# A fused scan and feed-forward kernel: masks of the second pair issued early, scores put into the differences' banks, two constants moved, one weight clamp issued ahead of a hidden block

## The chip, the cores and the metric

One core of a Trainium2 chip. The metric is the device time of one execution in microseconds; a median is of several executions. The engines are called PE (TensorE), DVE (VectorE), ACT (ScalarE), POOL (GpSimd) and SP (SyncE, which here only issues transfers).

## The reference, cut to what matters

A chunked state-space scan over 768 positions (4 batches, 8 heads of 32, state 16), whose output, reshaped to 3072 tokens of 256, goes through a feed-forward layer with a quick GELU:

```python
cum = np.cumsum(log(clip(a)), axis=-1)
L = np.exp(cum[..., :, None] - cum[..., None, :]) * causal
M = np.einsum('bhin,bhjn->bhij', Cc, Bc) * L          # scores times decays
y = M @ x + (C @ state) * exp(cum)                    # within and across chunks
...                                                    # state is carried from chunk to chunk
h = x @ w_in                                           # 256 x 2048
out = (h / (1 + exp(-1.702 * h))) @ w_out              # 2048 x 256
```

The weights are 64-bit floats. The kernel reads them as pairs of 32-bit words and makes 32-bit floats of them itself.

## The kernel before

The scan runs over pairs of 128-position chunks. For a pair, `mask` writes the causal mask into a PSUM bank, `differ` adds the differences of `cum` to it (32-row products, one group of rows per `r`), `decay_exp` takes the exponent on ACT, `score` computes C times B, `weigh` multiplies the two on DVE, `turn_only` transposes b and c, `ends` forms Be and `since_start` CsT (b and C weighted with decays), `gain` and `keep` advance the state, `finish` forms y.

```python
own = const.tile([P, HB, D], FP32, name="own")
nc.gpsimd.tensor_tensor(out=own, in0=same[:, :HB], in1=same[:, HB:], op=ALU.add)
idents = const.tile([P, NH, P], FP32, name="idents")
nc.gpsimd.tensor_copy(idents, ident.unsqueeze(1).to_broadcast([P, NH, P]))
```

A weight piece is decoded in four steps, three on DVE and one on ACT. Pieces 0 to 5 are `w_in`, 6 to 9 are `w_out`; piece 6 is the first 1 MB of `w_out`:

```python
def fields(i):   # DVE, L157 and L160: exponent bits, mantissa bits
def clamp(i):    # ACT, L168 and L169: two Relus over the exponent
def rounded(i):  # DVE, L173: adds the low word
def join(i):     # DVE, L184 and L190: sign, product into w_in or w_out
    ...
    for n in NEXT.get(i, ()):      # NEXT = {1: (6,), 4: (7,), 5: (8,), 7: (9,)}
        fetch(n)                   # loads piece n into the buffer that join(i) freed
def narrow(i):
    rounded(i); fields(i + 1); join(i)
```

All loads named here are issued by SP in program order:

```python
for i in range(1, 4): fetch(i)
rows_a(az, (nc.sync,))
for i in range(4, 6): fetch(i)
load(PG)              # b, c and x of the third pair: six strided loads
spread_rows(1)        # rows of a
# ... and, where join(1) stands in the program, fetch(6)
```

The start, with what the change touches:

```python
for r in range(R):
    ab[0, r] = ab0[:, r]; mask(ab[0, r])
idle = bank("idle")
for i in range(4):
    mask(idle)                       # filler: keeps PE busy, result unused
differ(0, ...); exps(0, range(R)); turn_only(0, ...)
fields(0); clamp(0); rounded(0)
score(0)
for r in range(2):
    ab[1, r] = bank(f"ab1_{r}"); mask(ab[1, r])
differ(1, ...); exps(1, range(2))
ends(0, 0, nc.gpsimd); ends(0, 1, nc.gpsimd)
weigh(0); turn_only(1, ...); gain(0)
...                                  # masks 2 and 3, differences, exponents
since_start(0, nc.gpsimd)            # CsT on POOL
since_start(1, nc.gpsimd)
keep(0); join(0); fields(1); rounded(1)
...                                  # score(1), weigh(1), y of pair 0
half(0, 0)                           # first half hidden block
weigh(1, (1,)); finish(1, late=True); join(1)
half(1, 0); keep(1, (1,))
fields(2); clamp(2)
load(PG + 1)
```

After that come the other half blocks (`half`), full hidden blocks 4 to 15 (`hidden`, L654), and the projection (`o`, L766), which needs `w_out`'s first piece decoded.

## Time and profile before

| | before |
|---|---|
| median | 377.97 us (3 runs, 377.84 to 378.61) |
| profiled span | 376.0 us, clock full |
| PE busy | 98% of the span |
| first scores | 10.38 us |
| first half hidden block | 20.42 us |
| block eight (behind PE's last wait of the first 60 us) | 37.66 us |
| block twelve | 46.70 us |
| first projection | 54.11 us |
| last PE operation | 371.52 us |

Between the two stands one more input, `w_out`'s first piece. These are SP's issues that lead to it (columns: start and duration in us, queue, line, operation):

```profile
17.46 6.48 SPq L119 DMA_DIRECT2D b<-in_B_dram  x2
23.98 3.89 SPq L119 DMA_DIRECT2D c<-in_C_dram  x2
27.92 1.25 SPq L119 DMA_DIRECT2D x<-in_x_dram  x2
29.21 0.79 SPq L222 DMA_DIRECT2D af<-in_a_dram  x1
30.13 0.37 SPq L145 DMA_DIRECT2D bits<-in_moe_w_out_dram  x1
```

The buffer for the piece is free once `join(1)` has read it, by 23.92 at the latest, but SP issues the load at 30.13, because until 29.17 it is at the third pair's b, c and x. Not all of that is issuing. SP's own waits from 12 to 34 us hold this line (total us, times, longest):

```profile
SPq L119 <- DMA bits<-in_moe_w_in_dram: 4.1, 2, 3.0
```

SP waits twice for an earlier piece of `w_in` to land, 1.1 us before b's first load and 3.0 between its two, so the 6.48 us above contain 3.0 of waiting. In the built program the loads count on eight semaphores in turn, and each waits until the load eight places ahead of it has landed. The piece landed at 38.44, and DVE's `fields(6)` started at 39.37 without a wait: 0.9 us of slack, which no list of waits shows.

### The profile page before, as it was taken

Reading aid. Unit: us, or ns where it says so; the run is one execution under the profiler, and the core shown is the slowest. Engines: PE = TensorE matmul, PEld = TensorE weight load, DVE = VectorE, ACT = ScalarE, POOL = GpSimd, SP = SyncE. Lnnn points to the kernel's source line nnn. Section 1 sums busy time; section 2 is a strip of 40 time slices with the busy share of each in tenths; the row PEclk is TensorE's granted clock in tenths of the full one; section 3 lists DMA queues with packets and bytes.
Section 4 is the critical chain, followed back from the end, with each engine's and each line's share of the span. In section 5 each row is a group of like instructions: output and inputs, shape, how many; then the busy total and the mean of one; then the engine's idle time right before and its main releaser. Section 6 shows DMA issues by size and latency. Waiting matters only on the chain.

```text
span 376.0 us, 5774 instructions
## 1 busy us (share of the span) xinstructions
PE 367.3 (98%) x2282; PEld 284.5 (76%) x2282; DVE 268.4 (71%) x439; ACT 152.2 (40%) x337; POOL 12.4 (3%) x35
## 2 busy tenths in 40 slices
PE   8999999999999999999999999999999999999995
PEld 3674458876457678878888878888878888888884
DVE  4889999996879998677887564888574355544343
ACT  5668643402332122554333454333454331454330
POOL 6200000000000010000000000000000000000000
PEclk9999999999999999999999999999999999999999
DMA  9989788624848100077300064000010000000011
GB/s 152 240 255 204 169 300 120 156 98 83 200 87 177 58 15 27 2 126 154 108 6 0 3 104 121 0 2 0 0 58 2 0 3 1 0 2 0 0 58 56
DMA packets 85795, 29.56 MB, mean 79 GB/s; under 512 B 75721, under 2 KB 79241, under 8 KB 85769
## 3 DMA queue, kind: packets, MB, share of 16 engines
q1 hardware_dynamic: 83320, 28.81, 32.9%
q10 hardware_dynamic: 2448, 0.39, 0.6%
q8 instruction: 18, 0.29, 0.3%
q14 instruction: 9, 0.07, 0.1%
HBM read 25.95 MB, written 3.24 MB: 78 GB/s over the span
## 4 chain that ended last, share of the span: by engine, by line
PE 93%; DVE 3%; ACT 2%; DMA 1%; issue 1%; ACTq 0%; DVEq 0%
PE acc L823 32%; PE X L726 15%; PE Y L736 11%; PE h L654 11%; PE o L766 8%; PE cb L539 3%; PE y L612 3%; PE y L603 2%; PE tp L496 2%; PE ab L460 1%; PE oT L857 1%; PE h L668 1%; PE A L567 1%; DMA az<-in_a_dram 1%; DVE p L184 1%
## 5 line engine op out<-in xcount | busy, mean ns | idle before, releaser
L823 PE MATMUL acc<-mg,mw 128*128 128x256 f32 x240 | 65.4, 379 | 0.0
L731 ACT ACTIVATE ac<-X 128x256 f32<-128x256 f32 x64 | 24.6, 384 | 68.9 <-PE X L726 68.8
L654 PE MATMUL h<-yT,w_in 128*128 128x512 f32 x112 | 50.3, 596 | 0.9 <-DVE w_in L190 0.8
L823 PEld LDWEIGHTS acc<-mg,mw 128*128 128x128 f32 x240 | 45.6, 190 | 6.2
L840 DVE TENSOR_TENSOR gT<-Y,ac 128x512 f32<-128x512 f32 x32 | 22.1, 692 | 38.0 <-PE Y L736 34.9
L703 ACT ACTIVATE gT<-gT 128x512 f32<-128x512 f32 x64 | 33.3, 520 | 28.5 <-DVE gT L840 28.5
L823 PE MATMUL acc<-gT,w_out 128*128 128x256 f32 x160 | 43.8, 380 | 0.0
L352 DVE TENSOR_TENSOR_SCAN L<-a,idents 128x1024 f32<-128x1024 f32 x18 | 41.1, 2283 | 0.0
L654 PEld LDWEIGHTS h<-yT,w_in 128*128 128x128 f32 x112 | 20.7, 190 | 24.9 <-issue 22.9
L726 PE MATMUL X<-my,mi 128*128 128x256 f32 x128 | 38.7, 384 | 0.0
L823 PEld LDWEIGHTS acc<-gT,w_out 128*128 128x128 f32 x160 | 30.1, 190 | 5.4 <-issue 1.4
L840 DVE TENSOR_TENSOR gT<-Y,b 128x256 f32<-128x256 f32 x32 | 13.5, 422 | 28.0 <-PE Y L736 27.7
L657 ACT ACTIVATE gT<-h 128x512 f32<-128x512 f32 x28 | 16.5, 596 | 39.7 <-PE h L654 39.7
L550 DVE TENSOR_TENSOR L<-L,cb 128x2048 f32<-128x2048 f32 (+1 forms) x13 | 27.6, 2121 | 5.7 <-PE cb L539 5.5
L766 PE MATMUL o<-w_out,gT 128*128 128x256 f32 x128 | 29.3, 383 | 0.0
L694 DVE TENSOR_TENSOR mg<-gT 128x512 f32<-128x512 f32 x40 | 27.3, 683 | 1.9 <-ACT gT L703 1.9
L726 PEld LDWEIGHTS X<-my,mi 128*128 128x128 f32 x128 | 23.8, 190 | 4.2 <-issue 1.2
L766 PEld LDWEIGHTS o<-w_out,gT 128*128 128x128 f32 x128 | 23.8, 190 | 4.1 <-issue 0.7
L823 PE MATMUL acc<-gT,mw 128*128 128x256 f32 (+1 forms) x86 | 24.0, 368 | 0.4 <-DVE c L840 0.4
L823 PE MATMUL acc<-mg,w_out 128*128 128x256 f32 x80 | 23.5, 379 | 0.0
L634 ACT ACTIVATE yT<-y 128x256 f32<-128x256 f32 x22 | 7.2, 381 | 36.7 <-PE y L612 35.5
L736 PE MATMUL Y<-yT,mi 128*128 128x256 f32 x64 | 19.5, 386 | 0.0
(142 smaller groups left out, 540.9 us busy)
## 6 DMA issues: line engine op xcount, KB each, us to landing
a<-scratch SPq DMA_DIRECT2D x18, 512.0 KB, 5.5
bits<-in_moe_w_out_dram SPq DMA_DIRECT2D x4, 1024.0 KB, 7.1
x<-in_x_dram SPq DMA_DIRECT2D x24, 128.0 KB, 3.1
out_dram<-ob SPq DMA_DIRECT2D x11, 256.0 KB, 2.2
bits<-in_moe_w_in_dram SPq DMA_DIRECT2D x4, 512.0 KB
bits<-in_moe_w_in_dram SPq DMA_DIRECT2D x2, 1024.0 KB
b<-in_B_dram SPq DMA_DIRECT2D x24, 64.0 KB, 3.8
c<-in_C_dram SPq DMA_DIRECT2D x22, 64.0 KB, 2.8
```

The costliest lines, as they stand in the source:

```text
L352: nc.vector.tensor_tensor_scan(out=Ls[p][:, k].rearrange("p r q i -> p (r q i)"), data0=ra[n], data1=idents.rearrange("p h i -> p (h i)"), ...
L550: nc.vector.tensor_tensor(out=Lv[:, k], in0=Lv[:, k], in1=cb.rearrange("p r k e -> p k r e")[:, k], op=ALU.mult)
L654: nc.tensor.matmul(out=h, lhsT=w_in[:, k, f * P:(f + 1) * P], rhs=yT[g][:, k], start=(k == 0), stop=(k == NK - 1))
L657: nc.scalar.activation(gT[g, j][:, i], h, AF.Silu, scale=GELU_SCALE)
L694: nc.vector.tensor_tensor(out=t[:, 0:2], in0=B[:, :, 1], in1=B[:, 0], op=ALU.subtract)
L703: nc.scalar.activation(o, i, AF.Silu, scale=GELU_SCALE)
L726: nc.tensor.matmul(out=s["X"], lhsT=lhsT, rhs=rhs, start=i == "1", stop=i == "4", skip_group_check=True)
L731: nc.scalar.activation(copy, s["X"], AF.Copy)
L736: nc.tensor.matmul(out=o, lhsT=lhsT, rhs=rhs, start=s.pop("new", False), stop=i != "5", skip_group_check=True)
L766: nc.tensor.matmul(out=o[k // 2][:, k % 2], lhsT=gT[g, f // 2][:, f % 2, k * P:(k + 1) * P], rhs=w_out[:, f], start=(f == 0 and k % 2 == 0 ...
L823: nc.tensor.matmul(out=acc[g][0][i][:, cols], lhsT=lhsT, rhs=rhs[:, cols], start=(j == 0 and i in (0, 2, 5, 6)), stop=(j == NF // 2 - 1), ...
L840: nc.vector.tensor_tensor(out=o, in0=v, in1=w, op=ALU.add)
```

## The change

Its intent: take the second pair's first two masks off PE's path between scores and differences by issuing them where filler products stood; write the first scores over the four banks of the first differences, with another order of row groups; move two POOL constants away from the start, where they hold up DVE's scans; and issue `clamp(2)` on ACT ahead of the half block's Silu.

```diff
     own = const.tile([P, HB, D], FP32, name="own")
-    nc.gpsimd.tensor_tensor(out=own, in0=same[:, :HB], in1=same[:, HB:], op=ALU.add)
     idents = const.tile([P, NH, P], FP32, name="idents")
-    nc.gpsimd.tensor_copy(idents, ident.unsqueeze(1).to_broadcast([P, NH, P]))
@@ score
-    def score(p):
+    def score(p, to=None):
-        cb = area(f"cb{p}").rearrange("p r (k e) -> p r k e", k=2)
-        for k in range(2):
-            for r in range(R):
+        cb = (area(f"cb{p}") if to is None else to).rearrange("p r (k e) -> p r k e", k=2)
+        for k, r in [(k, r) for r in range(R) for k in range(2)] if to is not None else [
+                (k, r) for k in range(2) for r in range(R)]:
@@ the start
+    for r in range(2):
+        ab[1, r] = bank(f"ab1_{r}")
+        mask(ab[1, r])
     idle = bank("idle")
-    for i in range(4):
+    for i in range(2):
         mask(idle)
@@
-    score(0)
-    for r in range(2):
-        ab[1, r] = bank(f"ab1_{r}")
-        mask(ab[1, r])
+    score(0, ab0)
     differ(1, [(r, ab[1, r]) for r in range(2)])
     exps(1, range(2))
+    nc.gpsimd.tensor_tensor(out=own, in0=same[:, :HB], in1=same[:, HB:], op=ALU.add)
@@
     since_start(1, nc.gpsimd)
+    nc.gpsimd.tensor_copy(idents, ident.unsqueeze(1).to_broadcast([P, NH, P]))
@@
     join(1)
+    fields(2)
+    clamp(2)
     half(1, 0)
     keep(1, (1,))
-    fields(2)
-    clamp(2)
```

In the changed kernel most lines below 331 have a number lower by three: L654 is L651, L766 is L763, L460 is L457. The decoding lines (L157 to L190) keep theirs.

More of the change, by code (lines that the diff above doesn't have):

```diff
@@ L529, in scores @@
         weigh(p)
-    def score(p):
+    def score(p, to=None):
         s = st[p]
         BT, CT = s.pop("BT"), s.pop("CT")
-        cb = area(f"cb{p}").rearrange("p r (k e) -> p r k e", k=2)
-        for k in range(2):
-            for r in range(R):
-                rows = slice(32 * r, 32 * r + 32)
-                nc.tensor.matmul(out=cb[:, r, k], lhsT=BT[rows, k],
-                                 rhs=CT[rows, k].rearrange("p q i -> p (q i)"),
-                                 start=True, stop=True, tile_position=(32 * r, 0),
-                                 skip_group_check=True)
+        cb = (area(f"cb{p}") if to is None else to).rearrange("p r (k e) -> p r k e", k=2)
+        for k, r in [(k, r) for r in range(R) for k in range(2)] if to is not None else [
+                (k, r) for k in range(2) for r in range(R)]:
+            rows = slice(32 * r, 32 * r + 32)
+            nc.tensor.matmul(out=cb[:, r, k], lhsT=BT[rows, k],
+                             rhs=CT[rows, k].rearrange("p q i -> p (q i)"),
+                             start=True, stop=True, tile_position=(32 * r, 0),
+                             skip_group_check=True)
         s["cb"] = cb
```

## The prediction

> **What bounds the kernel now.** I read the page first (TensorE, PE, is busy 98% of 376.0 us), then the list of PE's waits over the whole span, then the chain of waits of the first 60 us, then the timeline there. PE's waits:
>
> ```profile
> PE busy L378 <- DVE ones L258: 1.2, 1, 1.2
> PE h L654 <- DVE w_in L190: 0.8, 1, 0.8
> PE ab L460 <- DVE cum L292: 0.7, 1, 0.7
> PE cb L539 <- DVE C L503: 0.5, 1, 0.5
> PE h L668 <- ACT y L634: 0.4, 1, 0.4
> PE acc L823 <- DVE c L840: 0.4, 1, 0.4
> ```
>
> All but the last, which is in the tail, fall before 37.66 us. From there PE streams without a wait to the tail, so the change is worth exactly what it moves the eighth hidden block (the first L654 matmul after the 0.8 us wait, at 37.66), unless the earlier PE then meets a wait that was hidden. The chain of waits (start, us, what) that leads there:
>
> ```profile
> 10.38 1.15 PE cb L539 x16
> 11.52 0.54 PE ab L452 x2
> 12.06 1.93 PE ab L460 x16
> 13.99 0.59 PE tp L496 x4
> ...
> 24.27 1.94 PE h L668 x8
> 26.20 0.02 issue
> 26.23 0.60 ACT gT L672
> 26.82 0.62 ACT p L168
> 27.44 0.02 issue
> 27.47 0.73 ACT p L169
> 28.20 0.02 issue
> 28.22 0.70 DVE p L184
> ...
> 36.29 1.24 DVE w_in L190
> 37.52 0.14 issue
> 37.66 3.67 PE h L654 x8
> ```
>
> Two stretches matter. Up to 24 us PE itself sets the pace with small matmuls, two masks (L452) among them. From 26.2 us the chain leaves PE: ScalarE (ACT) does a Silu, only then the clamp of weight piece 2 (L168, L169), for which VectorE (DVE) idles 1.63 us at L184. DVE then decodes pieces 2, 3, 4 nearly without a gap until PE has to wait for piece 4.
>
> **What the Trainium skill says.** (1) "SBUF — State Buffer", section "SBUF: two separate sides": DVE and GpSimd (POOL) share one port pair under an exclusive lock, held for a whole instruction, against DVE operations with two SBUF inputs or in a two-port mode; the other blocks fully. The trace agrees:
>
> ```profile
> 5.12 0.46 POOL L331 TENSOR_TENSOR own<-same 128x128 f32<-128x128 f32 x1
> 5.22 2.28 DVE L292 TENSOR_TENSOR_SCAN cum<-carry,cum 128x256 f32<-128x256 f32 x2 [0.48 <-ACT cum L287]
> 5.52 1.43 POOL L334 COPY idents<-ident 128x1024 f32<-128x1024 f32 x1
> ```
>
> The two scans last 908 and 1452 ns by the view of their line, while a scan of the same size at 48.2 us, L447, takes 691 ns. The first is held about 0.22 us (by own), the second about 0.76 us (by idents). (2) "TensorEngine Tiling (Array Packing)", "Key Properties": changing the tiling mode drains TensorE. Here masks use all 128 rows and their neighbours 32-row tiles, so both edges of the masks cost. (3) "TensorE: Matmul & The Clock Gate", Part 3, says matmuls stay in strict order. This trace disagrees across row groups: the second scores (L539) start at 16.44, while differences (L460), earlier in program order on other row groups, still start at 16.64, 16.86 and 17.08. So a row group can run ahead of another. (4) "ScalarE: Activation LUTs", "What ACT_TABLE_LOAD costs", gives 1283 ns for a load; the one before the first y copies took 1.28 us. The change leaves it.
>
> **The change part by part.** The built instruction orders tell more than the diff.
>
> *Masks.* Filler products on identical operands become the second pair's first two masks: eight products before the first scan as before (4 + 2 + 2 instead of 4 + 4), two fewer in all. They finish before cum arrives (6.18 us), so moving them costs nothing. At 11.45 the two masks vanish. Rounds of 32-row passes start 0.216 us apart (16.43, 16.64, 16.86, 17.08 above). The scores' last round starts at 10.38 + 0.32 + 2 x 0.216 = 11.13 (first round 0.32 with its exposed load), so the differences can start at 11.34 rather than 11.99, and without their own 0.10 us of first-load gap: 0.65 + 0.10 = 0.75 us. The rest follows: transposes 13.17 (was 13.92), A 13.76, second half's differences 14.71, their exponents on ACT 16.74 to 17.83 (were 17.49 to 18.58). The loads for those transposes land near 12 us, early enough.
>
> *Scores into the differences' banks.* In the program before, these were already the same four banks, and the first score waited for the fourth exponent (10.32). In the changed program the wait has the same values. So no wait goes. The new order (two products of one row group in a row) puts up to four passes of one group ahead of the next; the overtaking seen at 16.44 covers just about that depth. I count 0.
>
> *own.* On POOL nothing stands between its old and new place: same position, 0.
>
> *idents.* From 5.52 to behind the second CsT on POOL (16.53 before, about 15.8 now). The second scan gets 0.76 us faster, which nobody waits for: its readers start at 8.71 (the rows product). At the new place DVE works without a gap on two-SBUF-input or two-port operations (join 0, fields 1, rounded 1). Join 0's last operation would end at 17.80 - 0.75 = 17.05, idents then holds the lock 0.8 us, and rounded(1) ends at about 19.27 instead of 19.20. So DVE loses there all of the 0.75 us that the masks gave it.
>
> *Result at the first hidden blocks.* A(1) waits for DVE's Be (19.6 + 0.07), the y copies for ACT (early now). First hidden matmul: A(1) last issued near 19.9, then a change of mode, about 20.0 instead of 20.42, so 0.4 earlier. The next hidden block (24.19 before) needs join 1, which ended at 23.92 and now ends at 23.99: about 24.05, so 0.15 earlier. The halves that follow run until 29.48 - 0.15 = 29.33.
>
> *fields(2), clamp(2) ahead of the half.* ACT does clamp 2 directly behind the y copies: 24.54 to 25.92, instead of 26.72 to 28.19 behind the Silu. DVE runs fields 2, state, rounded 2, fields 3 to 26.53 and then join 2 without the 1.63 us wait: done at 27.86 instead of 29.64. The first full hidden block starts at PE's own 29.33 (was 29.79). Clamp 3 stays behind the Silu of the half that PE ends near 28.0: clamp 3 is done at 29.94. Join 3 then runs 29.97 to 31.38 (was 32.77), rounded 4 and fields 5 to 33.72, join 4 (1.22 + 1.23) to 36.12 instead of 37.51. PE arrives at 29.33 + 6.94 = 36.27 (four blocks took 29.79 to 36.30 for the last start, plus 0.43); join 4 plus its 0.146 us latency is 36.27 as well. Block eight: 36.28 instead of 37.66, so 1.38 us earlier. The 0.8 us wait disappears; the rest is PE's own start.
>
> *Sum.* Masks +0.75, idents -0.6 (of its 0.83 on DVE, what PE feels), leaving 0.15 at 24 us; clamp order adds about 1.2; scores, own 0: total 1.38. Behind it the slacks are: first projection at 54.11 against join 6 done at 53.57 (0.54 us). DVE is one gapless chain there, and fields 6 needs w_out's first piece, which landed near 38.4 whatever PE does, so DVE may come only about 0.9 earlier: join 6 near 52.70 plus 0.15, against PE's 52.73. That may give back 0.1. I predict 1.3 us.
>
> **The rivals.** *A: the lock costs nothing.* If idents slips in while DVE reads PSUM (the weighing L550, one SBUF input), then DVE keeps its 0.75 and PE reaches block eight about 0.5 earlier still: 1.8 to 1.9 us, 376.1. Against: DVE reads SBUF twice for 2 us just when POOL is free. *B: the new score order breaks the overlap of row groups.* Sixteen passes of which each group's four run alone would take about 2.8 us instead of 1.15 (an estimate: 13 steps of 0.216, since only the edges overlap); the differences come about 1.6 later, the mask gain is lost and DVE's first weighing, which starts at 12.00 now, waits too. With the clamp order still helping: 378 to 378.5. Against: the overtaking above. *C: the gain is given back behind 38 us* by a w_out piece or its load: 0.3 to 0.6 us kept, 377.5. For: 0.54 us of slack, and DMA is 90% busy in many slices until 45 us. Against: the DVE chain moves earlier as well. *D: the decode was bound by loads, not by ACT*: pieces 4 and 5 landed near 25 and 27.5, their fields start at 28.4 and 32.4 in my sum, so no.
>
> **Range and chances.** Three runs of before lie within 0.8 us. Predicted 376.7 us: 377.97 less 1.3. A's end is 376.1 and C's 377.5, and noise is 0.3: low 375.8, high 377.6. 2% is 7.6 us, ten times what any part can move, so within 2% has 0.98, the sides 0.01 each.
>
> **What would show it.** Right: differences (L457 in the new numbering) straight behind the scores near 11.35 with no L449 between, transposes near 13.2; idents near 17 us with a DVE operation of 1.1 to 1.2 us beside it that takes 0.4 elsewhere; L184 of join 2 with no wait for ACT; the first hidden block near 20.0, block eight near 36.3; the wait of PE for w_in L190 gone or under 0.2; the distance from block eight to the end unchanged at 338.3 within 0.2. Wrong: scores lasting over 1.3 us (B); no lengthened DVE operation beside idents (A); a new wait of PE near 52.8 (C).

## The result, and the profile after

The changed kernel took 377.30 us in the median (6 runs, 376.50 to 377.86) against 377.96 (6 runs, 377.84 to 378.80) of the kernel before in the same rounds. The ratio is 0.9976, with a 95% interval of 0.9961 to 0.9991. All ratios here are the mean time of one kernel's fast runs over that of the other's fast runs of the same rounds, so not quite the ratio of the medians. The kernel is faster by 0.24%: 0.66 us by the medians, 0.92 by the means, where 1.3 us were predicted. The time lies inside the range.

| station, us | before | after | predicted | gain |
|---|---|---|---|---|
| first scores | 10.38 | 10.36 | 10.38 | 0.02 |
| first half hidden block | 20.42 | 19.98 | 20.0 | 0.44 |
| second half hidden block | 24.20 | 24.00 | 24.05 | 0.20 |
| first full block | 29.79 | 29.26 | 29.33 | 0.53 |
| block eight | 37.66 | 36.12 | 36.28 | 1.54 |
| block twelve | 46.70 | 45.09 | | 1.61 |
| first projection | 54.11 | 53.27 | about 52.85 | 0.84 |
| last PE operation | 371.52 | 370.75 | | 0.77 |

Up to block twelve the gain is there, and larger than predicted. Between block twelve and the first projection half of it disappears. First the parts that came out as planned. PE's timeline from the scores on (columns: start, duration, engine, line, operation; in brackets the idle time before and its releaser):

```profile
10.36 1.17 PE L536 MATMUL ab<-CT,BT 32*128 32x256 f32 x16 [0.55 <-DVE C L500]
11.33 1.03 PE L457 MATMUL ab<-cum,pick 32*128 32x256 f32 x8
12.19 1.04 PE L457 MATMUL ab<-minus,cum 32*128 32x256 f32 x8
13.16 0.44 PE L493 MATMUL tp<-ident,b 128*128 128x128 f32 x2
```

No mask stands between scores and differences, the differences start at 11.33 where the prediction has 11.34, and the transposes at 13.16 where it has 13.17. The reordered scores take 1.17 us instead of 1.15, so the row groups still overlap. On POOL and on DVE, one fence for each:

```profile
16.43 1.50 POOL L957 COPY idents<-ident 128x1024 f32<-128x1024 f32 x1
```

```profile
15.84 1.20 DVE L190 SCALAR_TENSOR_TENSOR w_in<-m,p 128x512 f32<-128x512 f32 x1
16.96 1.25 DVE L157 TENSOR_SCALAR p<-bits 128x512 uint32<-128x512 uint32 x1
```

`idents` starts at 16.43, finds DVE in L190, and lasts 1.50 us; it takes 1.03 where nothing holds it (experiment 9). The next DVE operation, L157, lasts 1.25 us where the same form took 0.42 in the kernel before. That is the lock on the shared port pair at work: one waits in the other's record. The moved clamp, on ACT and on DVE:

```profile
24.41 0.72 ACT L168 ACTIVATE p<-p,edge 128x512 f32<-128x512 uint32 x1
```

```profile
26.31 0.68 DVE L184 SCALAR_TENSOR_TENSOR p<-bits,p 128x512 uint32<-128x512 uint32 x1
```

The clamp of piece 2 starts at 24.41 (26.72 before), ahead of the half block's Silu, and `join(2)` starts at 26.31 without its wait of 1.63 us. Now what was not planned, PE's waits over the whole span (total us, times, longest):

```profile
PE busy L375 <- DVE ones L258: 1.2, 1, 1.2
PE o L763 <- DVE w_out L190: 0.6, 1, 0.6
PE ab L536 <- DVE C L500: 0.5, 1, 0.5
PE A L564 <- DVE Be L394: 0.5, 1, 0.5
...
```

The 0.8 us wait of the hidden blocks for L190 is gone, as intended; 0.2 us for L190 are left at the second half block. In its place stands a wait of the projection for `w_out`. DVE's own waits from 30 to 60 us tell why, together with the chain of waits there:

```profile
DVE p L157 <- DMA bits<-in_moe_w_out_dram: 1.1, 1, 1.1
```

```profile
30.85 8.04 DMA bits<-in_moe_w_out_dram
38.90 0.02 issue
38.92 0.69 DVE p L157
...
51.90 1.24 DVE w_out L190
53.13 0.14 issue
53.27 1.97 PE o L763 x8
```

DVE is ready for `fields(6)` near 37.8, the piece lands at 38.90, and from there DVE works without a pause until `join(6)` ends at 53.12. In the kernel before, the same chain contained no transfer here.

Two stretches have the same length in every trace, to 0.02 us. From `fields(6)` to the end of `join(6)` it is 14.20 us, and the projection follows 0.15 us later. From block twelve to the projection PE needs 7.41 us if it does not wait. So:

first projection = the later of (block twelve + 7.41) and (start of `fields(6)` + 14.35)

| kernel | block twelve + 7.41 | `fields(6)` + 14.35 | measured |
|---|---|---|---|
| before | 46.70 + 7.41 = 54.11 | 39.37 + 14.35 = 53.72 | 54.11 |
| changed | 45.09 + 7.41 = 52.50 | 38.92 + 14.35 = 53.27 | 53.27 |

Before, PE arrived last, by 0.39 us. After, the piece arrives last, by 0.77 us.

### The profile page after: what moved, and what is told of

Its sections match the earlier page's. It is cut to its first block, busy times and chain, and to the rows that moved or that the text cites. A ratio compares the mean times of both kernels' runs of the same rounds, so it can differ in the third digit from the quotient of the medians.

```text
span 375.2 us, 5771 instructions
## 1 busy us (share of the span) xinstructions
PE 367.2 (98%) x2280; PEld 284.8 (76%) x2280; DVE 268.2 (71%) x439; ACT 152.3 (41%) x337; POOL 12.4 (3%) x35
## 4 chain that ended last, share of the span: by engine, by line
PE 87%; DVE 8%; DMA 2%; issue 1%; ACT 1%; DVEq 0%; ACTq 0%
PE acc L820 32%; PE X L723 15%; PE Y L733 11%; PE o L763 8%; PE h L651 7%; PE cb L536 3%; PE y L609 3%; DMA bits<-in_moe_w_out_dram 2%; PE y L600 2%; PE tp L493 1%; DVE L L547 1%; DVE L L384 1%; PE oT L854 1%; DVE p L184 1%; PE h L665 1%
## 5 line engine op out<-in xcount | busy, mean ns | idle before, releaser
L651 PE MATMUL h<-yT,w_in 128*128 128x512 f32 x112 | 50.0, 595 | 0.0
L651 PEld LDWEIGHTS h<-yT,w_in 128*128 128x128 f32 x112 | 20.8, 190 | 23.4 <-issue 22.4
L654 ACT ACTIVATE gT<-h 128x512 f32<-128x512 f32 x28 | 16.6, 596 | 39.6 <-PE h L651 39.5
L763 PE MATMUL o<-w_out,gT 128*128 128x256 f32 x128 | 29.4, 384 | 0.6 <-DVE w_out L190 0.6
L547 DVE TENSOR_TENSOR L<-L,cb 128x2048 f32<-128x2048 f32 (+1 forms) x12 | 25.3, 2109 | 6.2 <-PE cb L536 6.2
L763 PEld LDWEIGHTS o<-w_out,gT 128*128 128x128 f32 x128 | 23.7, 190 | 4.9 <-issue 1.1
```

What stands on the lines that cost most here:

```text
L547: nc.vector.tensor_tensor(out=Lv[:, k], in0=Lv[:, k], in1=cb.rearrange("p r k e -> p k r e")[:, k], op=ALU.mult)
L651: nc.tensor.matmul(out=h, lhsT=w_in[:, k, f * P:(f + 1) * P], rhs=yT[g][:, k], start=(k == 0), stop=(k == NK - 1))
L654: nc.scalar.activation(gT[g, j][:, i], h, AF.Silu, scale=GELU_SCALE)
L763: nc.tensor.matmul(out=o[k // 2][:, k % 2], lhsT=gT[g, f // 2][:, f % 2, k * P:(k + 1) * P], rhs=w_out[:, f], start=(f == 0 and k % 2 == 0 ...
```

## The experiments

Twelve kernels ran: eight on one chip, in two sets, and the last four on a second one. All gave correct results. On the first chip the kernel before took 378.31 us (11 runs; 378.37 with the one run that the second set added), on the second 378.37 (11 runs). The theory after the result (call it L): the piece sets the end, because its load lands at about 39 us whatever the decoding does. The rival (call it S): the gain is eaten by something at the start, the lock that `idents` holds, or the new score order.

### 1. The rows of a later

Is the load of the piece slowed by the transfer just ahead of it?

```diff
 load(PG)
-spread_rows(1)
@@
 join(1)
+spread_rows(1)
```

> The changed kernel, but the 384 KB load of the rows of a (spread_rows) is issued behind the first w_out piece instead of ahead of it. Theory L (load): the changed kernel lost about 0.7 us of its head start at the first projection because fields 6 waits 1.1 us for that piece, which landed near 38.9 us. Then with the load moved: no wait of DVE for bits, PE's wait for w_out (0.6 us) gone or under 0.1, the first projection near 52.6 instead of 53.27, and the time 0.6 us under the changed kernel's: about 376.7. Rival C (DVE itself is the bound there, the load only fills its gap): the first projection stays within 0.2 of 53.27 and the time at 377.1 to 377.4.

Measured: 377.29 us (376.88 to 379.33), ratio 0.9984, interval 0.9964 to 1.0003. Nothing gained. Of the load's 16 parts 12 had landed by 36.73 us, 1.6 us earlier than in the changed kernel (38.31), but the last one came at 39.26, and that one releases DVE. DVE's waits from 30 to 75 us:

```profile
DVE p L157 <- DMA bits<-in_moe_w_out_dram: 3.7, 2, 2.5
```

The first is 1.2 us for this piece. The 2.5 us are for the third piece of `w_out`, which came late in this execution (56.98 in place of 54.09): from the projection to the last PE operation it took 317.96 us in place of 317.48. What follows: with the rows of a out of its way the last part still came at 39.26. Experiment 3 has the same edit without the second wait, and its piece landed at 39.09, no earlier than in the changed kernel. The Trainium skill, page "DMA: Bandwidth & Descriptors", section "Why a DMA increments its semaphore by 16 and not by 1", says that a transfer runs on up to 16 engines that finish independently and that only the full count means that all has landed. This trace agrees: DVE was ready at 38.06 and started at 39.28, behind the slowest of 16, which came 2.5 us behind the twelfth.

### 2. The constants back at the start

S tested: the changed kernel with `own` and `idents` where they were.

```diff
+nc.gpsimd.tensor_tensor(out=own, in0=same[:, :HB], in1=same[:, HB:], op=ALU.add)
+nc.gpsimd.tensor_copy(idents, ident.unsqueeze(1).to_broadcast([P, NH, P]))
@@ and taken out of their new places
```

> The changed kernel with own and idents built where the kernel before builds them. Both theories of the port lock: L157 of fields 1 takes 0.42 us instead of 1.25 and the first hidden blocks come earlier (the second one near 23.4 to 23.5 instead of 24.00), block eight near 35.6 instead of 36.13. Theory L: the end does not move, because the w_out piece still lands near 38.5 to 38.9; PE's wait for w_out grows from 0.6 to about 1.1 and the time stays at 377.1 to 377.4. Rival P (the end follows PE's start): 376.8.

Measured: 377.36 us (376.69 to 377.56), ratio 0.9974 (0.9962 to 0.9986), the same as the changed kernel. In the trace, the second half hidden block comes 13.07 us behind the first scores in place of 13.64, so the lock did cost 0.57 us there. But the piece landed at 39.1 and the projection started at 53.47 = 39.11 + 14.35 (+0.01). What follows: the lock's cost is real and does not reach the end. S falls for the size of the missing gain.

### 3. Both edits together

> Both edits of the two runs before together. Theory L: now both gains count, first projection near 52.1, time about 376.1 to 376.3, less than with either edit alone. Rival P: no more than the constants alone give (376.8).

Measured: 377.20 us (376.19 to 380.06), ratio 0.998 (0.9951 to 1.0008). The edits do not add up. The projection started at 53.46, again 14.35 behind `fields(6)` (39.11), although SP issued the piece at 29.46, 1.4 us earlier than in the changed kernel. In this execution a landed late and `idents` took the lock ahead of the first scan, of which more in experiment 7.

### 4. The old order of the scores

```diff
-for k, r in [(k, r) for r in range(R) for k in range(2)] if to is not None else [
-        (k, r) for k in range(2) for r in range(R)]:
+for k, r in [(k, r) for k in range(2) for r in range(R)]:
```

> The changed kernel with the first scores in the old order (all four row groups, then the second product of each), still in the differences' banks. My theory: no difference, scores 1.15 us within 0.05 either way, time equal to the changed kernel's 377.3 within its noise of 0.3. Rival: the new order is worth something, then scores or differences start over 0.1 us later here.

Measured: 377.46 us (377.14 to 378.55), ratio 0.9986 (0.9972 to 1.0001). The scores took 1.15 us in place of 1.17, and the differences started 0.96 us behind the scores' start in place of 0.97. The order is worth nothing either way. One more thing: this execution's first scores came 0.83 us later than the changed kernel's, and its block twelve too (45.92), yet its last PE operation started within 0.01 us of the changed kernel's. The start had 0.77 us to give away, as the second table says. Part of the delay is a late a (4.36 us in place of 4.09). The other part is PE's own: the eight mask and filler products ahead of the differences start 0.43 us apart at first and 0.22 later, and where the step comes differs from execution to execution. In experiments 1, 2, 4, 5 and 11 it did not come before the differences. In the last four of these the products ran past the end of the first scan, and the differences started 0.2 to 0.5 us late. (Here the way from the differences to the scores took 0.36 us longer as well.) Why the step moves, the traces do not show.

### 5. The first `w_out` piece early

The direct test of L. The piece needs no freed buffer: half of the final `w_out` tile, which nothing writes until much later, takes it. So its load can be issued right behind the last `w_in` piece, ahead of the third pair's loads.

```diff
-        if n == 2 and f % 4:
+        if i == 6:
+            t = w_out[:, 8:16].rearrange("p f e -> p (f e)").bitcast(U32)
+        elif n == 2 and f % 4:
@@
-    NEXT = {1: (6,), 4: (7,), 5: (8,), 7: (9,)}
+    NEXT = {4: (7,), 5: (8,), 7: (9,)}
@@
-    for i in range(4, 6):
+    for i in range(4, 7):
         fetch(i)
     load(PG)
```

> The changed kernel, with the first w_out piece read into the unused half of the final w_out tile, so that it needs no freed buffer, and issued straight behind the last w_in piece, ahead of the loads of b, c, x and of the rows of a. Theory L (behind block eight the end is set by the landing of this piece, through fields 6, join 6 and the first projection; in the changed kernel it landed at 38.9 and PE then waited 0.6 us): it should land near 28 to 31 us, DVE's wait at fields 6 (1.1 us) and PE's wait for w_out at the first projection go, the projection starts 0.5 to 0.6 earlier relative to the scores, and the time falls by 0.6 to about 376.7. Rival C (DVE is the bound behind block eight whatever is loaded): 377.1 to 377.4 as the changed kernel. Rival D (some other load becomes the wait, as the third w_out piece did when the rows of a were moved): a new DVE wait for bits of over 0.5 us at fields 7 or 8, and 377 or more.

Measured: 376.71 us (376.24 to 377.02), ratio 0.9957 (0.9944 to 0.9969), 0.6 us better than the changed kernel. The interval touches that of the changed kernel (0.9961 to 0.9991), so the trace has to decide. SP issued the piece at 18.87 instead of 30.85, and it landed at 30.58. PE's waits of this kernel, five groups in all, have no `w_out` in them (the two left out are those for Be and c, as in the changed kernel):

```profile
PE busy L377 <- DVE ones L260: 1.2, 1, 1.2
PE ab L538 <- DVE C L502: 0.5, 1, 0.5
...
PE h L667 <- DVE w_in L192: 0.2, 1, 0.2
```

The projection started at 52.97 = 45.56 + 7.41: PE's own arrival again. A later piece now makes DVE wait 1.5 us near 55 us, which PE does not feel. L holds.

### 6. The same with the constants back at the start

> The same with own and idents built where the kernel before builds them. Theory L: with the load out of the way the head start that idents costs (0.5 us at the second half block by its trace: 13.07 instead of 13.64 us behind the scores) now reaches the end: 0.4 to 0.5 under the run with the early piece alone, about 376.2. Rival P (the port lock costs the end nothing even then): equal to it.

Measured: 376.40 us (375.85 to 377.02, 4 runs), ratio 0.9952 (0.9937 to 0.9967). With the piece out of the way the lock's cost can reach the end. Counted from the first scores, the projection comes after 41.60 us in place of 42.15 in experiment 5. That is the 0.55 us of experiment 2. In the medians it is 0.3, and the intervals overlap, so the times alone do not settle it; the traces do.

### 7. The masks alone

The kernel before, with the two masks moved and nothing else.

> The kernel before with the masks' move alone. Second half block 0.75 earlier relative to the scores (13.07 us behind them instead of 13.82), block eight also 0.7 to 0.8 earlier, DVE at fields 6 about 0.75 earlier, that is near 38.6 and just at the landing of the w_out piece (38.4 to 39.1). Theory L: time 0.4 to 0.75 under before, nearly what the whole change gives. If parts simply added (rival): 0.75 here and 1.2 for the clamp, with -0.6 for idents.

Measured: 378.04 us (377.62 to 378.11, 4 runs) against 378.37, ratio 0.9993 (0.998 to 1.0006). Less than expected. Counted from the first scores, block eight came 0.76 us earlier than in the kernel before (26.52 us against 27.28), all that was expected. But in this execution the scores themselves came 0.88 us late. Two lines say why, one from POOL's timeline and one from DVE's:

```profile
5.43 1.03 POOL L334 COPY idents<-ident 128x1024 f32<-128x1024 f32 x1
```

```profile
5.65 1.94 DVE L292 TENSOR_TENSOR_SCAN cum<-carry,cum 128x256 f32<-128x256 f32 x2 [0.48 <-ACT cum L287]
```

The load of a landed at 4.42 us in place of 4.11, the first scan became ready at 5.65, and `idents` had already taken the lock at 5.43. So the first scan, which PE waits for, ran from 5.65 to 7.00, 1.35 us instead of 0.91. When a comes earlier, only the second scan is behind `idents`, and nobody waits for that one. In the two kernels of these runs with late a and the constants' `idents` moved away (experiments 1 and 4), the first scan took 0.69 us.

### 8. The clamp alone

The kernel before, with `fields(2)` and `clamp(2)` ahead of the half block.

> The kernel before with fields 2 and clamp 2 ahead of the half, alone. First half blocks unmoved, block eight 1.2 us earlier (36.4), PE's wait for w_in at block eight gone. Theory L: fields 6 then waits for the w_out piece, and only 0.4 to 0.9 of the 1.2 reaches the end; time 0.4 to 0.9 under before, with a PE wait for w_out of 0.3 to 0.7 at the first projection. Rival (parts add): 1.2 under before, 376.8.

Measured: 377.35 us (376.60 to 377.73, 4 runs), ratio 0.998 (0.9965 to 0.9995). One part of the change alone does, in the median, what the whole change does. Block eight came at 36.39, 1.27 us earlier. The projection started at 52.77, PE's own time, because the piece happened to land at 38.19, just as DVE was ready for it (38.09):

```profile
38.21 0.69 DVE L157 TENSOR_SCALAR p<-bits 128x1024 uint32<-128x1024 uint32 x1
```

So PE's expected wait for `w_out` is not in this trace, whose time of 376.60 is the lowest of the four. That the slower runs had the wait is likely, but not shown.

### 9. The piece early, and the constants in a slot where no lock is asked for

DVE's first weighing takes 2.27 us and reads one operand from PSUM. POOL is idle for most of it. So, on experiment 5, `own` and `idents` go between the two CsT:

```diff
     since_start(0, nc.gpsimd)
+    nc.gpsimd.tensor_tensor(out=own, in0=same[:, :HB], in1=same[:, HB:], op=ALU.add)
+    nc.gpsimd.tensor_copy(idents, ident.unsqueeze(1).to_broadcast([P, NH, P]))
     since_start(1, nc.gpsimd)
```

> The changed kernel with the early w_out piece, and own and idents both built by POOL right behind the first CsT, while DVE's first weighing (2.27 us, one SBUF input, the other in PSUM) runs, which by theory S takes no port lock. Theory S (a copy beside two-SBUF-input work costs, beside the weighing it is free, and at the very start it can block the first scan when a lands late, as it did in two profiles with the constants at the start: first scan 1.35 us): first scan 0.69 us or less, weighing 2.27 to 2.35 us, L157 of fields 1 takes 0.42 us, second half block 12.9 to 13.1 us behind the scores, no PE wait for w_out; time 375.8 to 376.2, a little under the run with the constants at the start (376.4). Rival (POOL blocks the weighing too): weighing over 2.8 us and no gain over the early piece alone (376.7).

Measured: 376.34 us (375.79 to 376.74, 5 runs), ratio 0.9944 (0.9931 to 0.9956), the lowest median of all, though a little over what was expected. POOL and DVE in that stretch:

```profile
12.57 0.45 POOL L957 TENSOR_TENSOR own<-same 128x128 f32<-128x128 f32 x1
12.97 1.03 POOL L958 COPY idents<-ident 128x1024 f32<-128x1024 f32 x1
```

```profile
12.22 2.27 DVE L549 TENSOR_TENSOR L<-L,ab 128x2048 f32<-128x2048 f32 x1
17.74 0.43 DVE L159 TENSOR_SCALAR p<-bits 128x512 uint32<-128x512 uint32 x1 [0.47 <-DMA bits<-in_moe_w_in_dram]
```

Both ran beside the weighing, and neither was stretched: 1.03 us for `idents` in place of 1.50, 2.27 for the weighing as before. In this execution DVE then waited 0.47 us for `w_in`'s second piece, so not all that the slot saves reached PE: the projection came 41.85 us behind the first scores, against 42.15 and 41.60 in experiments 5 and 6. In the medians the three differ by less than their ranges.

### 10. `idents` alone

The kernel before, with `idents` behind the second CsT.

> The kernel before with idents moved behind the second CsT, alone. Port lock: L157 of fields 1 takes 1.2 us, the second half block starts 0.5 to 0.7 later relative to the scores (14.4 us instead of 13.82), block eight and first projection likewise, because in this kernel DVE's decode, not the load, is the bound. From the profile alone: time 0.5 to 0.7 over before. Theory S: against that stands the first scan, which is no longer blocked in executions where a lands late, so the net is smaller: 0 to 0.5 over before. Rival (idents costs nothing): before or under.

Measured: 378.40 us (378.37 to 378.45, 5 runs) against 378.37, ratio 1.0000 (0.9988 to 1.0012). In the trace block eight comes 27.82 us behind the first scores in place of 27.28: the move costs 0.54 us there. Yet the median stands. The kernel before scatters in two clumps on that chip, 377.85 to 377.98 (4 runs) and 378.36 to 378.82 (7 runs), and this kernel sits with the second and does not scatter. That fits experiment 7: the old place is cheap when a lands early and dear when it lands late. That the clumps are this is an inference, since only profiled executions show when a landed, and it has a rival. In experiment 11, whose start is that of the kernel before, a landed early (3.84 us), yet the first scores came at 10.96 and the run took 378.52 us, in the second clump: PE's filler products ran until 6.62 (experiment 4).

### 11. The early piece without the change (control)

The kernel before with the edit of experiment 5.

> Control: the kernel before with the early w_out piece alone. In the kernel before, DVE never waits for that piece (it reaches fields 6 at 39.37, the piece lands near 38.4), so theory L says no change: within 0.3 of before, and the same 0.8 us wait of PE at block eight. If it is faster by 0.5 or more, the load costs something there that the profile of before does not show.

Measured: 378.41 us (377.93 to 378.82, 6 runs), ratio 0.9998 (0.9985 to 1.0011). The edit is worth nothing where the piece was not last. So the 0.6 us of experiment 5 come from the change's own gain let through.

### 12. The changed kernel again

> The changed kernel itself once more, on the chip of the runs above, so that it stands beside them: ratio to before 0.9961 to 0.9991 as the first time, w_out piece landing between 38.2 and 39.3, PE waiting 0.3 to 0.9 us for w_out at the first projection unless the start of the program was late.

Measured: 377.41 us (377.06 to 377.55, 5 runs), ratio 0.9973 (0.9961 to 0.9985). This time SP issued the piece at 31.55, it landed at 39.28, and the projection started at 53.66, while PE alone would have been there at 45.05 + 7.41 = 52.46 us. So 1.2 us were lost in this execution and 0.77 in the first; PE's wait for `w_out`, 1.0 us, is a little over the 0.3 to 0.9 expected.

### What the runs say together

Each part's gain at block eight, counted from each trace's first scores:

| part | us |
|---|---|
| masks (experiment 7) | 27.28 - 26.52 = +0.76 |
| `idents` (experiment 10) | 27.28 - 27.82 = -0.54 |
| clamp order (experiment 8) | 27.28 - 25.97 = +1.31 |
| sum | +1.53 |
| the whole change | 27.28 - 25.76 = +1.52 |

The formula for the projection holds in all of these to 0.02 us:

| experiment | block twelve + 7.41 | `fields(6)` + 14.35 | measured |
|---|---|---|---|
| 1 | 52.74 | 53.63 | 53.63 |
| 2 | 52.59 | 53.46 | 53.47 |
| 3 | 52.87 | 53.46 | 53.46 |
| 4 | 53.33 | 52.92 | 53.33 |
| 5 | 52.97 | 52.56 | 52.97 |
| 8 | 52.77 | 52.56 | 52.77 |
| 9 | 52.46 | 52.04 | 52.45 |
| 12 | 52.46 | 53.65 | 53.66 |

What stays open is why the piece lands when it does. Behind the third pair's loads SP issued it at 29.46 to 31.55 us, and it landed 7.7 to 9.6 us later, between 38.2 and 39.3 in ten traces. An earlier issue did not land earlier (experiment 3: issued at 29.46, landed at 39.1). Only the issue near 18 to 20 us, in experiments 5, 6, 9 and 11, took it out of the way: there it landed between 30.3 and 30.9. Whether the change itself delays the landing is not shown: it was 38.2 to 39.3 in the kernel before and experiments 7, 8 and 10, and 38.4 to 39.3 in the changed kernel and experiments 1 to 4.

## Why the prediction was right or wrong

- **Masks: +0.75 predicted, +0.76 found.** Right in mechanism and size, and in the moments that follow from it (11.34 and 13.17 predicted, 11.33 and 13.16 found). No run separates the masks' own time from the change of tiling mode around them. That the fillers "finish before cum arrives" was true of the trace that the prediction read, not of all (experiment 4).
- **Score order: 0 predicted, 0.02 us found** (1.17 against 1.15). Rival B, which had the row groups running one after the other, falls.
- **`own`: 0 predicted.** It ran at 5.10 us, where it had run at 5.12, and the first scan kept its 0.91 us.
- **`idents`: a DVE operation of 1.1 to 1.2 us beside it, -0.6 predicted; 1.25 us and -0.54 found.** The lock is right. Rival A, no cost, falls for the place where the change puts it. Its mechanism is real for another place: experiment 9 slipped `idents` in beside the weighing, free of charge.
- **"Second scan gets 0.76 us faster, which nobody waits for."** True of the execution that the prediction read, not of all. When a lands 0.2 to 0.3 us later the first scan takes that place (experiments 3 and 7). The step missed that an order between two engines can depend on a load's jitter.
- **Clamp order: about +1.2 predicted, +1.31 found.** ACT's clamp ended at 25.89 (25.92 predicted). DVE was even a little ahead of its plan, and block eight came at 36.12 instead of 36.28. Rival D falls too: `fields` of pieces 4 and 5 started without a wait, at 28.24 and 32.20.
- **What comes behind block eight: "That may give back 0.1."** This is the term of the sum that was mis-sized. It measured 0.77 us in the profiled execution and 1.2 in experiment 12. The mechanism, rival C, was named, with its cause, a `w_out` piece, and its sign came: a new wait of PE at the projection. The argument against it, "the DVE chain moves earlier as well", is what failed, because `fields(6)` could start no earlier than the landing. What was wrong was the number fed into it. The prediction took the landing at 38.4, from one trace, for a fixed moment and let DVE come 0.9 us earlier. The landing was 38.90 and 39.28, so `fields(6)` came 0.45 and 0.07 us earlier. Of a gain of 1.5 to 1.6 us at blocks eight and twelve, 0.84 us in the profile and 0.66 in the medians were left, and 0.96 in the medians of experiment 12 (378.37 to 377.41). The prediction said 1.3. That the time fell inside the range owes more to the range, whose upper end was set for rival C, than to the sum: 377.30 is 0.2 us from C's 377.5 and 0.6 from the 376.7 predicted.
- **The proof that this is the cause** is the pair of experiments 5 and 11: with the piece early the changed kernel gains 1.66 us on the kernel before in the medians (378.37 to 376.71), about the 1.54 us of block eight, while the kernel before gains nothing from the same edit.
- **"The distance from block eight to the end unchanged at 338.3 within 0.2"** did not hold. It grew to 339.1 us (375.2 less 36.12), which is the wait for the piece.

The prediction did list both slacks: 0.9 us on DVE, and 0.54 on PE, which is 0.39 when the 0.15 from `join(6)` to the projection is taken off. A wait that is absent only by so much is about to appear when the gain is 1.5. What was missing beside the slacks was the scatter of the load's landing.

## What to carry to other kernels

When a change moves a front forward by an amount G, list every input that the later work takes from a transfer, with its slack, and count as kept only what the smallest slack allows; a landing read from one execution is a sample (here 38.2 to 39.3 us), not a constant. Look also at where a load stands in its issuing queue: the piece's buffer was free 6 to 7 us before SP came to issue it, behind six strided loads that could come later without harm (experiment 5 issued them 2.0 to 2.6 us later than the changed kernel) and behind SP's own waits for earlier loads. And where GpSimd and VectorE share ports, try GpSimd's big copies beside a VectorE operation that reads PSUM: here the same copy cost 0.54 us in one place and stretched nothing in the other (experiment 9).

## What the Trainium skill lacked or had wrong

- "TensorE: Matmul & The Clock Gate", Part 3, has matmuls in strict order. The trace of the kernel before shows scores starting at 16.44 us, ahead of differences that stand earlier in program order and start at 16.64, 16.86 and 17.08 on other row groups.
- "SBUF — State Buffer", "SBUF: two separate sides", agrees with the runs on the lock: L157 took 1.25 us beside `idents` in place of 0.42, and the weighing, with one PSUM operand, took 2.27 with and without `idents` beside it. It gives the pair to whichever starts first, but does not add that the winner can change from run to run: a landing 0.3 us later made the first scan 1.35 us long instead of 0.91.
- "DMA: Bandwidth & Descriptors" says that a transfer's 16 parts finish independently. I found no figure in that section for how far apart they can be: in experiment 1, 12 parts had landed 2.5 us before the last.
- None of the pages consulted has a figure for single issues on this chip as long as some here. In the kernel before, SP's issue of the third pair's second b load took 3.03 us and of its first c load 3.27, where those of the other loads of that pair took 0.47 to 0.63. Why, the traces do not show.
